# Linear attention with a routed expert layer on one core: four weight chunks, the first rows and small counts placed anew at the turn from attention to the experts

## Chip, cores and metric

The kernel runs on one core of one Trainium2 chip. The metric is the device time of one execution in microseconds (us); the median of three executions counts. All times below are from the hardware's records of such executions.

## What is computed

The first half is a linear attention over 8 batches, 8 heads, 576 positions and 64 channels. The second half takes its output as 4608 tokens of width 512 and sends those with a positive skip score to one of 8 experts. Everything is float32. Cut to what matters:

```
proj = x @ w_phi; proj -= max|proj|          # for q and for k, 128 features
phi  = concat(exp(proj), exp(-proj))         # 256 features
num  = phi_q @ (phi_k^T v);  den = phi_q . sum(phi_k) + 1e-6
x    = (num / den), heads side by side       # [4608, 512]
skip = x @ w_skip > 0;  e = argmax(x @ w_gate);  g = softmax(x @ w_gate)[e]
out  = x;  out[skip] = x + g * (relu(x @ w1[e]) @ w2[e])   # w1 512x1024, w2 1024x512
```

## The kernel before

**Attention.** A loop over time steps `t` runs two streams of units (k and q), one batch after another. TensorE projects and multiplies, VectorE subtracts the maxima, transposes inputs and divides by `den` (lines 490 to 504), ScalarE takes the exponentials, and GpSimd adds partial sums. The order on TensorE, ScalarE and VectorE is the order of the program text nearly to the end of attention; the last steps are ordered by a planner.

**Routing.** After each batch b, `post(b)` makes four things. `choose` picks the expert of each token (one-hot `OH`), its weight through an exponential on ScalarE (line 657) and the reciprocal of its sum on VectorE (line 665), and then stores the right half of the token rows to `xrows` in DRAM (`store_rows`, lines 625 and 627, on SP's queue). `rank` counts the tokens of each expert so far with matmuls over `Stot` and `OH` (line 681 is the first), and `turned` makes from it 128x128 masks `OP` (line 709: two per tile of tokens), on GpSimd for all batches but the last, where VectorE makes them. After batch 5 (`EB`), `pick(0)` and `pick(1)` choose the first two experts from what is counted so far: they subtract the chosen tokens from `Stot` (line 797) and gather 256 rows each from `xrows` with two indirect DMAs on GpSimd's queue (line 213). VectorE's small steps of these generators are slipped in one at a time between the large ones (`hook`); a `yield` is the border of such a step. A third expert is picked later by `pick_third`, in three steps.

**Experts.** The weights come in chunks of 128x1024 float32 through SP's queue (lines 184 and 187): four chunks of `w1`, then four of `w2` for each expert. I number them from one, so chunk one is index 0 in the code. Four buffers take the first twelve chunks. A chunk is split into a high part, written by ScalarE (line 195), and a low part, the difference, written either by VectorE in one instruction or by GpSimd in four pieces of 256 columns (line 200); `CFG['gp']` lists the indices that GpSimd takes. The buffer is free for the next load when both are written. The gathered rows are transposed by TensorE (line 955) and split in the same way into `x` by ScalarE and VectorE (lines 958 and 959). A step of the expert loop is one chunk: `mm1` (lines 1081 to 1084, three products of high and low parts; ScalarE's Relu on line 973, VectorE's difference on line 974) or `mm2` (lines 1095 to 1100). At each step the loop first queues what `before` holds, then splits of coming chunks and the loads behind them, then the matmuls, then what `at` put on that step: the steps of `pick_third` on steps 1 to 3, the last batch's `rank` on step 4, and the steps of `tables` from step 5. One step after an expert's last chunk, VectorE adds the weighted result to the rows (line 1042) and GpSimd scatters them to the output (line 1028).

**Before the loop** stand the loads of chunks one to four, the two gathers, `rows` of the first expert, the splits of chunks one to four with `choose` of the last batch ahead of the fourth, and `rows` of the second expert. There the planner orders the instructions; `tc.issue_after(ins)` only queues what is traced in its block behind `ins`, and only on the engine of `ins`. In the loop the order is that of the program. Before, the last lines ahead of the loop are:

```
if k == FIRST - 1:
    with tc.issue_after(row_last[1].ins):
        for _ in chosen[0]: pass          # choose() of the last batch
...
part(k, nc.gpsimd if k in CFG["gp"] else nc.vector)
rows(order[1])
```

Of the kernel before, what the change touches and what calls it, by code (L numbers as in the profile page):

```python
# [12 lines left out]
AF = mybir.ActivationFunctionType  # L13
ALU = mybir.AluOpType
# [3 lines left out]

P = 128
SLOT = 256  # L20
CFG = {'late': 1, 'gp': (0, 1, 2, 4, 6, 8, 9, 11, 12, 14, 17, 19, 21), 'rows': 9.0, 'tab': (2, 4, 5, 6, 6, 7, 8, 9, 10, 11, 12, 13, 16, 20, 32), 'ql': -2, 'q1': 0, 'vtl': 3, 'at': 6, 'cp': 0, 'seq': ('E', 'E', 'E', 'C', 'C', 'SC', 'C', 'DS', 'C', 'D'), 'lag': (1, 3, 4, 5, 6), 'post': (4, 7, 7), 'man': (8, 79), 'dnow': 0, 'off': 6, 'order': 'EPAZUT', 'direct': (), 'nb': {'K': 1, 'P': 3, 'U': 2, 'O': 2}, 'na': {'K': 1, 'P': 2, 'U': 1, 'O': 2}, 'apools': (('ld', 2), ('hl', 5), ('up', 3), ('zp', 2), ('ep', 7), ('kvp', 6), ('ac', 1), ('xp', 2)), 'mpools': (('rawp', 1), ('mx', 2), ('wseta', 1), ('mo', 2), ('wsetb', 1), ('rawq', 1))}


@with_exitstack
def kernel(
# [12 lines left out]
    nc = tc.nc  # L38
    B, H, S, D = q.shape
    NF = w_phi.shape[1]  # L40
    E = w_gate.shape[1]
# [14 lines left out]
    EB = B - 3  # L56
# [17 lines left out]
    ac = pools["ac"]  # L74
# [38 lines left out]
    Stot = const.tile([P, E], BF16, name="Stot")  # L113
# [145 lines left out]
    with actx:  # L259
        ld, hl, zp, up, ep, kvp, xp = (pools[nm] for nm in ("ld", "hl", "zp", "up", "ep", "kvp", "xp"))  # L260
# [337 lines left out]
        def post(b):  # L598
            last = b == B - 1
# [8 lines left out]
            nt = 4 if b % 2 == 0 else 5  # L608
# [3 lines left out]
            mx = sm("mx", [5])  # L612
            d = sm("d", [5, E])
            ex = sm("ex", [5, E + 1])
# [14 lines left out]
            def choose():  # L629
                for xx, lg, o, n in reversed(parts):  # L630
                    nc.vector.tensor_reduce(
                        out=L[:, o:o + n, :], in_=lg.rearrange("p t h e -> p t e h"), axis=AX.X, op=ALU.add,
                    )
                    yield
                nc.vector.tensor_reduce(out=mx[:, 0:nt], in_=L[:, 0:nt, 0:E], axis=AX.X, op=ALU.max)
                yield
                eng = nc.vector if last else nc.gpsimd
                eng.memset(ex[:, 0:nt, E:E + 1], 1e-9)
                eng.tensor_tensor(out=d[:, 0:nt], in0=L[:, 0:nt, 0:E], in1=bc(mx[:, 0:nt], nt, E), op=ALU.subtract)
                dr = desc.rearrange("p (o e) -> p o e", o=1).broadcast_to([P, nt, E])  # L640
                if last:
                    nc.vector.scalar_tensor_tensor(
                        out=key[:, 0:nt], in0=d[:, 0:nt], scalar=0.0, in1=dr, op0=ALU.is_equal, op1=ALU.mult)
                else:
                    nc.gpsimd.tensor_scalar(out=key[:, 0:nt], in0=d[:, 0:nt], scalar1=0.0, scalar2=None, op0=ALU.is_equal)
                    nc.gpsimd.tensor_tensor(out=key[:, 0:nt], in0=key[:, 0:nt], in1=dr, op=ALU.mult)
                    for _ in range(3):
                        yield
                nc.vector.tensor_reduce(out=km[:, 0:nt], in_=key[:, 0:nt], axis=AX.X, op=ALU.max)
                yield  # L650
                nc.vector.tensor_tensor(out=oh[:, 0:nt], in0=key[:, 0:nt], in1=bc(km[:, 0:nt], nt, E), op=ALU.is_equal)
                yield
                nc.vector.scalar_tensor_tensor(
                    out=OH[:, T, :], in0=L[:, 0:nt, E:E + 1].broadcast_to([P, nt, E]), scalar=0.0, in1=oh[:, 0:nt],
                    op0=ALU.is_gt, op1=ALU.mult,
                )
                nc.scalar.activation(out=ex[:, 0:nt, 0:E], in_=d[:, 0:nt], func=AF.Exp)
                for xx, lg, o, n in parts:
                    nc.scalar.activation(
                        out=xx[:, :, 4 * D + 1:4 * D + 2], in_=sid[:, t0 + o:t0 + o + n].rearrange("p (t o) -> p t o", o=1), func=AF.Copy)  # L660
                yield
                nc.vector.tensor_reduce(out=ss[:, 0:nt], in_=ex[:, 0:nt], axis=AX.X, op=ALU.add)
                yield
                for xx, lg, o, n in parts:
                    nc.vector.reciprocal(out=xx[:, :, 4 * D:4 * D + 1], in_=ss[:, o:o + n].rearrange("p (t o) -> p t o", o=1))
                store_rows()
# [9 lines left out]
            def rank():  # L676
# [3 lines left out]
                r = bank("K" if last else "O")[:, 0:nt * E]  # L680
# [13 lines left out]
                def turned():  # L694
                    if last:
                        count()
                    rm = sm("rm", [5, E])
                    rki = sm("rki", [5], I32)
                    rkp = sm("rkp", [5], I32)
                    nc.vector.tensor_tensor(  # L700
                        out=rm[:, 0:nt], in0=r.rearrange("p (t e) -> p t e", e=E), in1=OH[:, T, :], op=ALU.mult)
                    yield
                    with nc.allow_low_precision(reason="sums of integers below 2**24 written as integers"):
                        nc.vector.tensor_reduce(out=rki[:, 0:nt], in_=rm[:, 0:nt], axis=AX.X, op=ALU.add)
                    yield
                    nc.vector.tensor_scalar(out=rkp[:, 0:nt], in0=rki[:, 0:nt], scalar1=127, scalar2=None, op0=ALU.bitwise_and)  # L706
                    for c in range(2):
                        for t in range(nt):
                            (nc.vector if last else nc.gpsimd).tensor_scalar(  # L709
                                out=OP[:, t0 + t, c, :], in0=iota_p, scalar1=rkp[:, t:t + 1],  # L710
                                scalar2=wcol[:, NT:NT + 1] if c else wcol[:, t0 + t:t0 + t + 1], op0=ALU.is_equal, op1=ALU.mult)
                    yield
                    nc.vector.tensor_scalar(
                        out=RKH[:, T], in0=rki[:, 0:nt], scalar1=7, scalar2=None, op0=ALU.arith_shift_right)
                    yield
                    if not last:
                        count()
                        yield
                    if b > EB:
                        return  # L720
                    for s in range(S):
                        nc.vector.scalar_tensor_tensor(
                            out=rm4[:, 0:nt, :, s], in0=bc(RKH[:, T], nt, E), scalar=float(s), in1=OH[:, T, :],
                            op0=ALU.is_equal, op1=ALU.mult,
                        )
                        if s % 2 == 1:
                            yield
# [46 lines left out]
        def pick(j):  # L774
# [5 lines left out]
            def chosen_pair():  # L780
                mx = sm("mx", [5])[:, 0:1]
# [10 lines left out]
                    out=eid0[:, j:j + 1], in0=km[0:1], scalar1=-1.0, scalar2=float(E), op0=ALU.mult, op1=ALU.add)  # L792
                cs = sm("cs", [E])
                nc.vector.scalar_tensor_tensor(out=cs, in0=cn, scalar=float(SLOT), in1=pk, op0=ALU.min, op1=ALU.mult)
                r = slice(32 * j, 32 * j + 1)
                with nc.allow_low_precision(reason="integers up to 256 are exact"):
                    nc.gpsimd.tensor_tensor(out=Stot[r], in0=Stot[r], in1=cs[r], op=ALU.subtract)
                a4 = acc4.rearrange("p (e s) -> p e s", s=4)
                a2 = acc.rearrange("p (e s) -> p e s", s=2)
                po = pk.rearrange("p (e o) -> p e o", o=1).broadcast_to([P, E, 2])  # L800
# [1 line left out]
                ea = sm("ea", [2], bufs=1)  # L802
                nc.gpsimd.tensor_tensor(
                    out=tp.rearrange("p s e -> p e s"), in0=(a2 if j else a4)[:, :, 0:2], in1=po, op=ALU.mult)
                for _ in range(3):
                    yield
                nc.vector.tensor_reduce(out=ea, in_=tp, axis=AX.X, op=ALU.add)
                places(idg0[:, j], pad0[:, j], ea)
# [8 lines left out]

        rests = []
        chosen = []
        later = []  # L820
        now = [0]
        streams = []
# [7 lines left out]
        man = ExitStack()  # L830
# [455 lines left out]
    def rows(x):  # L1286
        kind, i = x
        xss[x] = split_rows(xgs[x], pad0[:, i] if kind == "E" else ft[:, i, 2:4])


    FIRST = 4
# [16 lines left out]
    def at(k, f):  # L1308
        along.append((k, f))
# [5 lines left out]
    rows(order[0])  # L1315
    for k in range(FIRST):

        if k == FIRST - 1:
            with tc.issue_after(row_last[1].ins):
                for _ in chosen[0]:  # L1320
                    pass
        with ExitStack() as es:
            if k:
                es.enter_context(tc.issue_after(kva_last[0].ins))
            if k == FIRST - 1:
                es.enter_context(tc.issue_after(row_last[0].ins))
                es.enter_context(tc.issue_after(row_last[1].ins))
            part(k, nc.gpsimd if k in CFG["gp"] else nc.vector)
    rows(order[1])
    table = tables()  # L1330
    parts = []

# [2 lines left out]
    one_done = {x: max(k for k, (w, y, c) in enumerate(steps) if y == x and w == 1) for x in order}  # L1335
    TAB = CFG["tab"]
    third = pick_third()
    for k in range(1, 4):
        at(k, lambda: next(third, None))
    at(TAB[1], rests[0])  # L1340
# [114 lines left out]
```

## Time and profile before

| | us |
|---|---|
| median of 3 executions | 590.76 |
| lowest and highest | 590.70, 592.84 |
| the profiled execution | 592.79 |
| its span | 591.0 |
| TensorE busy in the span | 552.0 |
| VectorE busy | 491.4 |
| GpSimd busy | 376.6 |
| ScalarE busy | 327.7 |

The span runs from the first to the last instruction of the profiled execution; 1.8 us of that execution's time lie around it. Starts below are counted from the start of the span. Attention ends and the experts begin at about 320 us.

### The profile page before, as it was taken

The numbers are of one execution on the slowest core, as the hardware profiler recorded it, in microseconds if no ns is written. First come the engines' busy times: TensorE is split into PE (matmuls) and PEld (weight loads), VectorE is DVE, ScalarE is ACT, GpSimd is POOL, SyncE is SP. The second block draws the span as 40 slices with busy tenths as digits, with TensorE's granted clock in tenths as the row PEclk, the third lists the DMA queues.
The fourth block names the chain that finished last, engine by engine and source line by source line (L and its number), as shares of the span: only waits on it lengthen the run. The fifth ranks groups of instructions, "written<-read, shape, count | busy, mean of one in ns | idle before, by whom it ended". The sixth has DMA issues, their size and how long they took to land. (4 is left out here: it accounts for less than half of the span.)

```text
span 591.0 us, 18778 instructions
## 1 busy us (share of the span) xinstructions
PE 552.0 (93%) x7486; PEld 467.6 (79%) x7486; DVE 491.4 (83%) x1056; ACT 327.7 (55%) x649; POOL 376.6 (64%) x434
## 2 busy tenths in 40 slices
PE   5799999999999999999997887999999999999993
PEld 3488888887887878878766867898899988988892
DVE  5789999999999989999876989657779887867840
ACT  4356666665665656556646243444658567546720
POOL 5656468688596794966946655974658582648031
PEclk9999999999999999999999899899999999999998
DMA  8998889697685986813153594788687778877400
GB/s 147 164 159 152 195 185 200 160 188 149 119 212 121 193 168 113 217 46 119 38 183 116 144 366 162 246 290 271 204 284 238 264 261 292 272 214 257 173 20 31
DMA packets 250298, 108.34 MB, mean 183 GB/s; under 512 B 192481, under 2 KB 235617, under 8 KB 250208
## 3 DMA queue, kind: packets, MB, share of 16 engines
q1 hardware_dynamic: 244640, 97.45, 63.3%
q0 software_dynamic: 3200, 9.45, 4.3%
q8 instruction: 60, 0.98, 0.7%
q10 hardware_dynamic: 2368, 0.22, 0.3%
q14 instruction: 30, 0.25, 0.1%
HBM read 83.86 MB, written 24.02 MB: 183 GB/s over the span
## 5 line engine op out<-in xcount | busy, mean ns | idle before, releaser
L200 POOL TENSOR_TENSOR w<-wraw_c,w 128x256 fp32r<-128x256 f32 x108 | 97.1, 931 | 46.6 <-ACT w L195 46.5
L398 POOL TENSOR_TENSOR z<-ek 128x512 f32<-128x512 f32 x64 | 80.8, 1275 | 67.2 <-ACT ek L391 57.7
L200 DVE TENSOR_TENSOR w<-wraw_c,w 128x1024 fp32r<-128x1024 f32 x69 | 98.2, 1439 | 8.8 <-ACT w L195 8.4
L195 ACT ACTIVATE w<-wraw_c 128x1024 fp32r<-128x1024 f32 x96 | 97.8, 1051 | 11.4 <-DMA wraw_c<-in_moe_w_dram 11.4
L370 DVE TENSOR_REDUCE m<-ps_P 128x8 f32<-128x1024 f32 (+3 forms) x86 | 89.6, 1041 | 7.1 <-PE ps_P L357 6.5
L374 DVE TENSOR_TENSOR u<-ps_P,m 128x1024 f32<-128x1024 f32 (+3 forms) x86 | 90.3, 1050 | 4.6
L357 PE MATMUL ps_P<-wsrc,xT 64*64 64x128 f32 x2048 | 72.4, 280 | 10.7 <-DVE xT L334 5.9
L569 PEld LDWEIGHTS ps_O<-kva,eq 128*64 128x64 f32 x2048 | 71.6, 136 | 6.3 <-PE ps_U L412 0.6
L357 PEld LDWEIGHTS ps_P<-wsrc,xT 64*64 64x64 f32 x2048 | 57.9, 135 | 21.2 <-issue 6.9
L569 PE MATMUL ps_O<-kva,eq 128*64 128x74 f32 x2048 | 72.9, 227 | 0.8 <-DVE lgm L504 0.4
L1028 POOL DMA_INDIRECT out_dram<-o,si x22 | 30.4, 1381 | 59.0 <-DVE si L1027 52.4
L434 PE MATMUL ps_K<-ek,v 128*64 128x256 f32 x512 | 67.5, 394 | 0.3 <-ACT ek L391 0.3
L1095 PE MATMUL ps_O<-w,hh 128*128 128x512 f32 x160 | 64.5, 403 | 0.0
L709 POOL TENSOR_SCALAR OP<-iota_p,rkp,wcol 128x128 bf16<-128x128 f32 x62 | 48.3, 793 | 10.6 <-DVE rkp L706 10.5
L418 ACT ACTIVATE eq<-ps_U 128x512 f32<-128x512 f32 x49 | 29.4, 600 | 42.6 <-PE ps_U L412 41.0
L434 PEld LDWEIGHTS ps_K<-ek,v 128*64 128x64 f32 x512 | 34.2, 139 | 20.7 <-issue 7.5
L390 ACT ACTIVATE ek<-u 128x512 f32<-128x512 f32 x64 | 41.2, 644 | 11.5 <-DMA wgs<-in_moe_w_skip_dram 6.3
L1099 PE MATMUL ps_O<-w,hh 128*128 128x512 f32 x120 | 47.4, 395 | 0.0
L1100 PE MATMUL ps_O<-w,hlo 128*128 128x512 f32 x120 | 47.3, 394 | 0.0
L334 DVE STREAM_TRANSPOSE xT<-raw 128x512 f32<-128x512 f32 x64 | 42.7, 685 | 3.1 <-DMA raw<-in_k_dram 3.1
L404 POOL TENSOR_TENSOR z<-z,ekt 64x512 f32<-64x512 f32 x32 | 40.7, 1272 | 1.8
L402 POOL TENSOR_TENSOR z<-z 128x512 f32<-128x512 f32 x32 | 40.6, 1275 | 1.3
(264 smaller groups left out, 1209.3 us busy)
## 6 DMA issues: line engine op xcount, KB each, us to landing
wraw_c<-in_moe_w_dram SPq DMA_DIRECT2D x96, 512.0 KB, 5.0
raw<-in_q_dram SPq DMA_DIRECT2D x64, 144.0 KB, 3.5
raw<-in_k_dram SPq DMA_DIRECT2D x60, 144.0 KB, 3.6
v<-in_v_dram SPq DMA_DIRECT2D x64, 128.0 KB, 3.2
out_dram<-xm SPq DMA_DIRECT2D x16, 512.0 KB, 4.7
xrows<-xm SPq DMA_DIRECT2D x8, 516.0 KB, 4.9
xrows<-xm SPq DMA_DIRECT2D x8, 512.0 KB, 4.3
vt<-in_v_dram SPq DMA_DIRECT2D x32, 32.0 KB, 3.3
```

Source lines behind the costliest of these rows:

```text
L195: nc.scalar.activation(out=hi, in_=raw, func=AF.Copy)
L200: eng.tensor_tensor(out=lo[:, r], in0=raw[:, r], in1=hi[:, r].bitcast(F32), op=ALU.subtract)
L357: nc.tensor.matmul(p[s * 64:s * 64 + 64, hd, (nj + j) * NF:(nj + j + 1) * NF], xT[r, g * P + s * 64:g * P + s * 64 + 64], wsrc[r], start=T ...
L370: nc.vector.tensor_reduce(out=m.rearrange("p (j h) -> p j h", h=2), in_=pv, axis=AX.X, op=ALU.max, apply_absolute_value=True)
L374: nc.vector.tensor_tensor(out=uu[:, 0:2 * nj, :].rearrange("p (j h) f -> p j h f", h=2), in0=pv, in1=m.rearrange("p (j h o) -> p j h o", h ...
L398: zeng.tensor_tensor(out=z, in0=e[:, 0:2, :], in1=e[:, 2:4, :], op=ALU.add)
L434: nc.tensor.matmul(o[hd * 64:hd * 64 + 64, :], u.v[:, 2 * hd + pr, g * D:(g + 1) * D], u.e[i][:, 2 * j + hd, :], start=(g == 0), stop=False,)
L569: nc.tensor.matmul(ov[s * 64:s * 64 + 64, 2 * j + hd, :], e[:, half, j, hd, s * 64:s * 64 + 64], kva[:, half, 2 * pr + hd, :], start=(half ...
L709: (nc.vector if last else nc.gpsimd).tensor_scalar(out=OP[:, t0 + t, c, :], in0=iota_p, scalar1=rkp[:, t:t + 1], scalar2=wcol[:, NT:NT + 1 ...
L1095: nc.tensor.matmul(y[sub], hh[:, t], wh[:, fi, :], start=first, stop=False)
L1099: nc.tensor.matmul(y[sub], hh[:, t], wl[:, fi, :], start=False, stop=False)
L1100: nc.tensor.matmul(y[sub], hlo[:, t], wh[:, fi, :], start=False, stop=last)
```

## The change

Of chunks one to four, GpSimd splits the first and the fourth, and VectorE the second and the third; before, GpSimd split the first three and VectorE the fourth. The splits on VectorE are queued behind the first expert's last row split, and ScalarE's parts of chunks three and four behind the first expert's rows and behind the exponential of the last batch's `choose`. That `choose` is now ahead of chunk three. The second expert's rows move into the expert loop, to the end of step 4, ahead of the last batch's `rank`. VectorE subtracts from `Stot` in both picks, the second pick waits one small step in place of three, and of the eight masks of the last batch but one VectorE makes two.

```diff
-CFG = {'late': 1, 'gp': (0, 1, 2, 4, 6, 8, 9, 11, 12, 14, 17, 19, 21), ...
+CFG = {'late': 1, 'gp': (0, 3, 4, 6, 8, 9, 11, 12, 14, 17, 19, 21), ...
...
-                nc.scalar.activation(out=ex[:, 0:nt, 0:E], in_=d[:, 0:nt], func=AF.Exp)
+                ex_last[0] = nc.scalar.activation(out=ex[:, 0:nt, 0:E], in_=d[:, 0:nt], func=AF.Exp)
...
-                            (nc.vector if last else nc.gpsimd).tensor_scalar(
+                            (nc.vector if last or b > EB and t == 0 else nc.gpsimd).tensor_scalar(
...
-                    nc.gpsimd.tensor_tensor(out=Stot[r], in0=Stot[r], in1=cs[r], op=ALU.subtract)
+                    nc.vector.tensor_tensor(out=Stot[r], in0=Stot[r], in1=cs[r], op=ALU.subtract)
...
-                for _ in range(3):
+                for _ in range(3 - 2 * j):
                     yield
...
-        if k == FIRST - 1:
+        if k == 2:
             with tc.issue_after(row_last[1].ins):
                 for _ in chosen[0]:
                     pass
         with ExitStack() as es:
             if k:
                 es.enter_context(tc.issue_after(kva_last[0].ins))
-            if k == FIRST - 1:
+                es.enter_context(tc.issue_after(row_last[1].ins))
+            if k >= 2:
                 es.enter_context(tc.issue_after(row_last[0].ins))
-                es.enter_context(tc.issue_after(row_last[1].ins))
+                es.enter_context(tc.issue_after(ex_last[0].ins))
             part(k, nc.gpsimd if k in CFG["gp"] else nc.vector)
-    rows(order[1])
...
+    at(4, lambda: rows(order[1]))
     for k in range(1, 4):
         at(k, lambda: next(third, None))
```

## Rows read from the trace of the kernel before

**Rows 1.** Busy time by stretch: microseconds, busy per engine, granted TensorE clock, DMA

```profile
330.00:340.00 10.00, 8.16 (x55) 7.92 (x55) 9.15 (x21) 3.59 (x6) 4.21 (x7) 0.83 0.57 161
...
360.00:370.00 10.00, 6.58 (x40) 5.69 (x40) 9.38 (x24) 2.61 (x4) 8.62 (x11) 0.87 0.36 127
370.00:380.00 10.00, 10.00 (x39) 8.28 (x39) 7.70 (x12) 4.50 (x5) 9.51 (x11) 0.79 0.61 195
...
470.00:480.00 10.00, 10.00 (x52) 8.28 (x51) 8.28 (x16) 7.08 (x14) 7.22 (x8) 1.00 0.92 338
```

**Rows 2.** Timeline of TensorE: start, duration, instruction, idle before and its releaser

```profile
314.04 0.18 PE L681 MATMUL ps_O<-Stot,ones_b 128*128 128x32 bf16 x1 [1.57 <-POOL Stot L797]
...
322.64 0.38 PE L1081 MATMUL ps_P<-x,w 128*128 128x256 f32 x1 [1.31 <-ACT x L958]
...
335.42 0.39 PE L1081 MATMUL ps_P<-x,w 128*128 128x256 f32 x1 [1.84 <-DVE hlo L974]
...
345.00 0.19 PE L681 MATMUL ps_K<-Stot,ones_b 128*128 128x40 bf16 x1 [2.20 <-DVE tp_e L253]
...
353.57 0.28 PE L1081 MATMUL ps_P<-x,w 128*128 128x256 f32 x1
...
366.10 0.38 PE L1084 MATMUL ps_P<-x,w 128*128 128x256 f32 x1 [1.33 <-POOL w L200]
...
368.05 0.58 PE L1084 MATMUL ps_P<-x,w 128*128 128x256 f32 x1 [0.60 <-POOL w L200]
```

**Rows 3.** Timeline of GpSimd, the same columns

```profile
313.80 0.19 POOL L797 TENSOR_TENSOR Stot<-Stot,cs 1x8 bf16<-1x8 bf16 x1 [5.47 <-DMA xg<-xrows,idg]
...
316.84 6.22 POOL L709 TENSOR_SCALAR OP<-iota_p,rkp,wcol 128x128 bf16<-128x128 f32 x8
323.04 8.35 POOL L200 TENSOR_TENSOR w<-wraw_c,w 128x256 fp32r<-128x256 f32 x12
...
361.16 1.09 POOL L1028 DMA_INDIRECT out_dram<-o,si  x1 [6.12 <-DVE si L1027]
...
363.58 7.47 POOL L200 TENSOR_TENSOR w<-wraw_c,w 128x256 fp32r<-128x256 f32 x8
```

**Rows 4.** Timeline of VectorE, the same columns

```profile
315.72 0.17 DVE L692 TENSOR_TENSOR Stot<-Stot,st 128x8 bf16<-128x8 bf16 x1
...
324.13 8.34 DVE L200 TENSOR_TENSOR w<-wraw_c,w 128x1024 fp32r<-128x1024 f32 x1
...
332.50 1.27 DVE L959 TENSOR_TENSOR x<-ps_U,x 128x512 fp32r<-128x512 f32 x2
...
337.82 1.74 DVE L200 TENSOR_TENSOR w<-wraw_c,w 128x1024 fp32r<-128x1024 f32 x1
...
343.44 0.69 DVE L974 SCALAR_TENSOR_TENSOR hlo<-ps_P,hh 128x512 fp32r<-128x512 f32 x1 [2.34 <-ACT hh L973]
...
345.80 1.21 DVE L200 TENSOR_TENSOR w<-wraw_c,w 128x1024 fp32r<-128x1024 f32 x1
...
348.00 5.73 DVE L709 TENSOR_SCALAR OP<-iota_p,rkp,wcol 128x128 bf16<-128x128 f32 x10
...
360.05 0.75 DVE L1042 SCALAR_TENSOR_TENSOR o<-ps_O,xg 128x512 f32<-128x512 f32 x1
```

**Rows 5.** Waits of VectorE from 343 to 372 us: total, times, longest

```profile
DVE hlo L974 <- ACT hh L973: 2.3, 1, 2.3
DVE w L200 <- ACT w L195: 0.2, 1, 0.2
```

**Rows 6.** Timeline of ScalarE, the same columns

```profile
318.66 2.95 ACT L195 ACTIVATE w<-wraw_c 128x1024 fp32r<-128x1024 f32 x3
...
341.87 1.06 ACT L195 ACTIVATE w<-wraw_c 128x1024 fp32r<-128x1024 f32 x1 [4.37 <-DMA wraw_c<-in_moe_w_dram]
```

**Rows 7.** Timeline of SP's queue, the same columns

```profile
334.70 0.37 SPq L625 DMA_DIRECT2D xrows<-xm  x1
...
335.89 1.35 SPq L187 DMA_DIRECT2D wraw_c<-in_moe_w_dram  x2
```

More of the change, by code (lines that the diff above doesn't have):

```diff
@@ L20 @@
 SLOT = 256
-CFG = {'late': 1, 'gp': (0, 1, 2, 4, 6, 8, 9, 11, 12, 14, 17, 19, 21), 'rows': 9.0, 'tab': (2, 4, 5, 6, 6, 7, 8, 9, 10, 11, 12, 13, 16, 20, 32), 'ql': -2, 'q1': 0, 'vtl': 3, 'at': 6, 'cp': 0, 'seq': ('E', 'E', 'E', 'C', 'C', 'SC', 'C', 'DS', 'C', 'D'), 'lag': (1, 3, 4, 5, 6), 'post': (4, 7, 7), 'man': (8, 79), 'dnow': 0, 'off': 6, 'order': 'EPAZUT', 'direct': (), 'nb': {'K': 1, 'P': 3, 'U': 2, 'O': 2}, 'na': {'K': 1, 'P': 2, 'U': 1, 'O': 2}, 'apools': (('ld', 2), ('hl', 5), ('up', 3), ('zp', 2), ('ep', 7), ('kvp', 6), ('ac', 1), ('xp', 2)), 'mpools': (('rawp', 1), ('mx', 2), ('wseta', 1), ('mo', 2), ('wsetb', 1), ('rawq', 1))}
+CFG = {'late': 1, 'gp': (0, 3, 4, 6, 8, 9, 11, 12, 14, 17, 19, 21), 'rows': 9.0, 'tab': (2, 4, 5, 6, 6, 7, 8, 9, 10, 11, 12, 13, 16, 20, 32), 'ql': -2, 'q1': 0, 'vtl': 3, 'at': 6, 'cp': 0, 'seq': ('E', 'E', 'E', 'C', 'C', 'SC', 'C', 'DS', 'C', 'D'), 'lag': (1, 3, 4, 5, 6), 'post': (4, 7, 7), 'man': (8, 79), 'dnow': 0, 'off': 6, 'order': 'EPAZUT', 'direct': (), 'nb': {'K': 1, 'P': 3, 'U': 2, 'O': 2}, 'na': {'K': 1, 'P': 2, 'U': 1, 'O': 2}, 'apools': (('ld', 2), ('hl', 5), ('up', 3), ('zp', 2), ('ep', 7), ('kvp', 6), ('ac', 1), ('xp', 2)), 'mpools': (('rawp', 1), ('mx', 2), ('wseta', 1), ('mo', 2), ('wsetb', 1), ('rawq', 1))}
 @with_exitstack
@@ L819 @@
         chosen = []
+        ex_last = [None]
         later = []
```

## Prediction

> **What bounds the kernel now.** I began with busy time by stretch [rows 1]. In the eleven windows of 10 us from 370 to 480 (the first and the last stand there, none is below 9.75) TensorE is always busy; ahead of them two windows miss 1.84 and 3.42 us. So the experts run at TensorE's pace once they run, and what the turn loses is not won back. The granted clock is below 1.00 in the same stretches: 0.83, 0.87 and 0.79, time at 1.2 instead of 2.4 GHz.
>
> TensorE's timeline [rows 2] names the waits: 1.57 us for GpSimd's subtraction from `Stot`, 1.31 for the first rows, 1.84 and 2.20 for small VectorE results, and last the stretch up to 368.05, where each piece of a low part on GpSimd is waited for. This last wait counts, since nothing behind it is idle. Followed back it gives a chain:
>
> - The pieces are those of chunk twelve, at 363.58, right behind the first expert's scatters at 361.16, which waited 6.12 us for VectorE [rows 3].
> - VectorE comes to these rows (line 1042) at 360.05. From 343.44 it has stood still only once, for 0.2 us [rows 4, 5]: its queue is full, and whatever starts it at 343.44 sets the end.
> - At 343.44 it waited 2.34 us for ScalarE, whose Relu stood behind the high part of chunk seven, which waited for its load until 341.87 [rows 4, 6].
> - That load was issued at 335.89, behind the row stores of the last batch at 334.70 [rows 7]. The stores need the last reciprocal of `choose`.
> - `choose` stood behind one split on VectorE, of chunk four: 8.34 us from 324.13, where the same instruction takes 1.21 at 345.80 [rows 4]. GpSimd's twelve pieces of chunks one to three ran from 323.04 for 8.35 us [rows 3]; VectorE was done 1.1 us behind the last of them.
>
> So an excess of 8.34 - 1.21 = 7.1 us on VectorE is carried, wait by wait, to 368.05.
>
> **The change part by part.**
>
> *Subtraction from `Stot` on VectorE.* GpSimd's took 0.19 us, but began 5.47 us late: it waited for the landing of the first gather [rows 3]. On VectorE the nearest row is the addition to the same tile, 0.17 us [rows 4]. Neither operand is what the gather writes, so I take the wait to go with GpSimd's queue, and TensorE's 1.57 us with it [rows 2]. If the wait moves along, VectorE stands up to 5.47 us with the last divisions of attention queued behind it: bounds 0.17 and 5.6 us.
>
> *The second pick two steps earlier* issues its gather earlier on a queue that no longer waits; its rows are needed in step 4 only. Worth nothing, covered by the first four chunks; without that cover it could cost at most the 5.47 us again.
>
> *Two masks on VectorE.* GpSimd's eight take 6.22 us, 0.78 each [rows 3]; six end 1.6 us earlier. VectorE's cost 5.73 / 10 = 0.57 each [rows 4], so 1.15 us ahead of the last divisions. Of TensorE's 1.57 us I therefore keep 1.0 at the end of attention (bounds 0.4 and 1.57).
>
> *First rows ahead of chunk three.* ScalarE made three high parts in 2.95 us before these rows [rows 6]; now two, 0.98 less. Together with the 1.0 the first rows are split some 1.7 us earlier (not 2.0, as TensorE's transposes must also have come).
>
> *The splits.* GpSimd has chunk one only in this stretch, 8.35 / 3 = 2.8 us, nearly all of it done before VectorE's split of chunk two. `choose` runs in a gap of GpSimd, since ScalarE makes chunks three and four only behind its exponential. VectorE gets one split more, 1.21 us. Its excess of 7.1 us goes. Two bounds: in a short overlap with four pieces a split took 1.74 us [rows 4], 0.5 more; against a row of pieces without end it stands for the whole row, 2.8 us for chunk four and as much again for chunk five.
>
> Here a page of the Trainium skill differs from the trace. The row shows a split held through twelve GpSimd instructions. "SBUF — State Buffer", section "Who interferes with whom", says that a VectorE instruction with two SBUF inputs and a GpSimd instruction that reads SBUF exclude each other for the whole of one instruction. By that the split would have waited for one piece, 0.7 us, and there would be no 7.1 us to win; the measured 8.34 decides. The rule speaks against the change where it puts VectorE's splits beside GpSimd's chunks four and five; by it they would lose 0.7 us each there, which lies inside the bounds of my case.
>
> *Start of the loads.* The stores at 334.70 came after the excess, the second rows' pair of splits (1.27 us, now moved away) and the choice. They are now earlier by 1.7 + 7.1 + 1.3, less the two splits that now stand ahead of them, 2.4: 7.7 us; chunk three's buffer is free in the same microsecond. The load of chunk seven moves with the stores. Bounds: 6 (0.5 lost at each of three overlaps) and 9 (load ahead of the stores, which saves their 1.2 us on SP [rows 7]). Its transfer keeps 341.87 - 335.89 = 6.0 us, in which stores share the DMA as before.
>
> *Second rows in step 4.* On TensorE they fall where it now waits for the third pick. On ScalarE they are covered. On VectorE they come into the full queue: 1.27 us [rows 4], unless they slip into the wait for the Relu, which they can't, as they are queued behind the third pick. VectorE works through to line 1042 as before.
>
> *Sum at 368.05:* -7.7 + 1.3 = -6.4. TensorE itself comes earlier, since the waits of 1.31, 1.84 and part of 2.20 us go too, and only waits longer for chunk twelve. The slow clock around 368 I leave as it is; if one stretch of it goes, [rows 1] give 0.13 x 10 to 0.21 x 10 us more. So -6.4, with -4.5 to -9 for this case. The profiled execution of 592.79 (span 591.0 and 1.8 around it) would become 586.4. It lies 2.0 above the median of 590.76; the prediction is for the median: **584.4 us**, 581.8 to 586.3.
>
> **The rivals.**
>
> *A shorter gain: chunk three's split is locked out again.* Its high part and that of chunk four come from ScalarE one after the other, 0.98 us apart. If VectorE reaches its split after GpSimd began on chunk four, it may stand for that row, 2.8 us, or through chunk five too, 5.6. For it: the row of 8.34. Against it: `choose` leaves VectorE little to do in just that microsecond. The `Stot` wait moved to VectorE falls here too. Gain 6.4 - 2.8 = 3.6 or 0.8: 587.2 or 590.0.
>
> *No change: the new wait is the load.* If SP's planner keeps the load of chunk seven behind something that has not moved, or its transfer meets the output stores that also come earlier, VectorE still starts at about 343 and the excess turns into idle time. For it: VectorE did idle 2.34 us there. Against: the load's row follows the stores within 1.2 us. Time 590.5.
>
> *Slower: VectorE's queue is longer.* Place: from the last divisions to line 1042. The added split 1.21, masks 1.15 and moved rows 1.27 make 3.6 us on the queue that sets the end. It decides where the locked-out time reaches the 7.1 us that it was before: chunk one's row for the split of chunk two, and four and five for chunk three, 3 x 2.8 = 8.4 us. Then the sum is 8.4 - 7.1 + 3.6 = 4.9, less the 1.7 of the earlier start: +3.2, 594.0. For it: GpSimd's pieces before stood in just such a row. Against it: between chunk one and chunk four GpSimd must wait for the exponential.
>
> **How the numbers follow.** The main case 0.62, the shorter gain 0.19, no change 0.10, slower 0.09. A measurement of this kernel tells about 0.5%, 3.0 us, from no change. Faster by more: 0.62 and two thirds of 0.19, 0.74; within: the rest of that and 0.10, 0.16; slower: 0.09, rounded up to 0.10. The range runs from 580.5 (the bound of 9 with a stretch of the slow clock) to 590.0 (the shorter gain's far end) and leaves out "no change", "slower" and little else, about 2 in 10.
>
> **What the profile of the changed kernel would show.** No wait of TensorE for `Stot`; VectorE's two first splits at 1.2 to 1.8 us each; row stores on SP near 327 and the load of chunk seven within 2 us behind them; VectorE's line 974 after its longest wait near 336; line 1042 near 354; TensorE at the last piece of chunk twelve near 361.7, after a longer wait there than before. A split of 3 us or more means the shorter gain. Line 1042 still near 360 means no change. The prediction is wrong if the wait for chunk twelve is set by something else than VectorE's queue, or if TensorE is no longer unbroken behind it.

## The result and the profile after

The changed kernel takes 586.55 us (median of five, 585.3 to 587.32) against 590.76 of the kernel before (five runs of the same occasion, 589.98 to 592.84): ratio 0.991, 95% interval 0.9883 to 0.9937. By the ratio it is faster by 0.9%, some 5.3 us; the two medians lie 4.2 us apart. 584.4 was predicted, with a range of 580.5 to 590.0 that holds the result; the likeliest case's own range ended 0.25 us below it, at 586.3. The profiled execution took 587.23, its span is 585.5. Behind line 820 the lines of the changed kernel are one higher: 1043 is 1042 of before.

Busy time by stretch, the columns of [rows 1]:

```profile
330.00:340.00 10.00, 10.00 (x77) 9.36 (x76) 8.27 (x24) 5.79 (x8) 8.06 (x11) 1.00 0.91 266
340.00:350.00 10.00, 10.00 (x56) 8.48 (x55) 9.59 (x30) 4.25 (x4) 5.76 (x8) 1.00 1.01 352
350.00:360.00 10.00, 7.99 (x65) 7.58 (x63) 9.52 (x30) 5.58 (x7) 4.90 (x7) 1.00 0.63 225
360.00:370.00 10.00, 9.05 (x34) 7.50 (x35) 9.62 (x20) 4.50 (x5) 9.51 (x11) 0.66 0.56 185
370.00:380.00 10.00, 10.00 (x60) 8.76 (x59) 6.24 (x10) 4.04 (x5) 9.59 (x11) 1.00 0.74 257
```

TensorE no longer misses anything from 330 to 350; what it misses now lies from 350 to 362. The 0.83 of 330 to 340 has gone with the waits there. The slow clock behind 360 has not: one window at 0.66 (3.4 us lost in granted clock) stands for 0.87 and 0.79 in [rows 1] (1.3 + 2.1).

The rows that answer the chain, from its start. VectorE, to be held against [rows 4]:

```profile
308.80 0.16 DVE L797 TENSOR_TENSOR Stot<-Stot,cs 1x8 bf16<-1x8 bf16 x1
...
316.39 0.66 DVE L709 TENSOR_SCALAR OP<-iota_p,rkp,wcol 128x128 bf16<-128x128 f32 x2
...
323.77 1.28 DVE L200 TENSOR_TENSOR w<-wraw_c,w 128x1024 fp32r<-128x1024 f32 x1
...
327.03 0.13 DVE L665 RECIPROCAL xt<-ss 128x1 f32<-128x1 f32 x1
...
327.58 1.23 DVE L200 TENSOR_TENSOR w<-wraw_c,w 128x1024 fp32r<-128x1024 f32 x1 [0.31 <-ACT w L195]
...
336.35 0.69 DVE L975 SCALAR_TENSOR_TENSOR hlo<-ps_P,hh 128x512 fp32r<-128x512 f32 x1 [0.83 <-ACT hh L974]
...
339.54 1.29 DVE L960 TENSOR_TENSOR x<-ps_U,x 128x512 fp32r<-128x512 f32 x2
...
341.81 3.15 DVE L709 TENSOR_SCALAR OP<-iota_p,rkp,wcol 128x128 bf16<-128x128 f32 x10
...
353.77 0.75 DVE L1043 SCALAR_TENSOR_TENSOR o<-ps_O,xg 128x512 f32<-128x512 f32 x1
```

Both first splits take what such a split takes alone, and the last reciprocal of `choose` ends between them, at 327.2. SP's queue [rows 7] follows it:

```profile
327.15 0.37 SPq L625 DMA_DIRECT2D xrows<-xm  x1
...
328.83 3.08 SPq L187 DMA_DIRECT2D wraw_c<-in_moe_w_dram  x2
```

GpSimd [rows 3]: six masks, one chunk, a pause until ScalarE has made the high part, and the scatters 6.28 us earlier.

```profile
316.46 4.75 POOL L709 TENSOR_SCALAR OP<-iota_p,rkp,wcol 128x128 bf16<-128x128 f32 x6 [4.01 <-DVE rkp L706]
321.19 2.78 POOL L200 TENSOR_TENSOR w<-wraw_c,w 128x256 fp32r<-128x256 f32 x4
328.57 9.48 POOL L200 TENSOR_TENSOR w<-wraw_c,w 128x256 fp32r<-128x256 f32 x12 [4.61 <-ACT w L195]
...
354.88 1.09 POOL L1029 DMA_INDIRECT out_dram<-o,si  x1 [5.11 <-DVE si L1028]
...
357.30 7.49 POOL L200 TENSOR_TENSOR w<-wraw_c,w 128x256 fp32r<-128x256 f32 x8
```

TensorE [rows 2]: the wait for `Stot` is gone and so are those of 1.84 and 2.20 us; three gaps that the profile puts down to nothing ("issue") have come; the wait for chunk twelve still stands last, its last piece at 361.79.

```profile
307.92 0.77 PE L465 MATMUL ps_O<-aug,kvs 128*128 128x146 f32 x4 [0.71 <-issue]
...
312.29 0.40 PE L548 MATMUL ps_O<-kva,eqt 128*64 128x74 f32 x5 [0.38 <-issue]
313.01 0.38 PE L548 MATMUL ps_O<-kva,eqt 128*64 128x74 f32 x5 [0.32 <-issue]
...
314.51 0.19 PE L681 MATMUL ps_O<-Stot,ones_b 128*128 128x32 bf16 x1
...
323.07 0.39 PE L1082 MATMUL ps_P<-x,w 128*128 128x256 f32 x1 [0.74 <-ACT x L959]
...
359.84 0.42 PE L1085 MATMUL ps_P<-x,w 128*128 128x256 f32 x1 [1.35 <-POOL w L200]
...
361.79 0.58 PE L1085 MATMUL ps_P<-x,w 128*128 128x256 f32 x1 [0.41 <-POOL w L200]
```

### The profile page after: what moved, and what is told of

Its sections match the earlier page's. It is cut to its first block, busy times and chain, and to the rows that moved or that the text cites. A ratio compares the mean times of both kernels' runs of the same rounds, so it can differ in the third digit from the quotient of the medians.

```text
span 585.5 us, 18767 instructions
## 1 busy us (share of the span) xinstructions
PE 550.1 (94%) x7486; PEld 465.8 (80%) x7486; DVE 488.0 (83%) x1061; ACT 328.2 (56%) x649; POOL 375.4 (64%) x426
## 5 line engine op out<-in xcount | busy, mean ns | idle before, releaser
L200 DVE TENSOR_TENSOR w<-wraw_c,w 128x1024 fp32r<-128x1024 f32 x70 | 92.7, 1339 | 8.7 <-ACT w L195 8.3
L370 DVE TENSOR_REDUCE m<-ps_P 128x8 f32<-128x1024 f32 (+3 forms) x86 | 89.6, 1042 | 7.1 <-PE ps_P L357 6.7
L1029 POOL DMA_INDIRECT out_dram<-o,si x22 | 31.6, 1434 | 56.1 <-DVE si L1028 49.2
L709 POOL TENSOR_SCALAR OP<-iota_p,rkp,wcol 128x128 bf16<-128x128 f32 x60 | 46.8, 794 | 14.5 <-DVE rkp L706 14.5
```

The costliest lines, as they stand in the source:

```text
L200: eng.tensor_tensor(out=lo[:, r], in0=raw[:, r], in1=hi[:, r].bitcast(F32), op=ALU.subtract)
L370: nc.vector.tensor_reduce(out=m.rearrange("p (j h) -> p j h", h=2), in_=pv, axis=AX.X, op=ALU.max, apply_absolute_value=True)
L709: (nc.vector if last or b > EB and t == 0 else nc.gpsimd).tensor_scalar(out=OP[:, t0 + t, c, :], in0=iota_p, scalar1=rkp[:, t:t + 1], scal ...
```

## Experiments

Each was timed in five rounds against the kernel before. "In us" is the ratio's distance from 1 on 590.76.

| kernel | median | ratio, interval | in us |
|---|---|---|---|
| the change, again | 586.09 | 0.9899, 0.9875 to 0.9922 | -6.0 |
| splits and order only | 587.75 | 0.9934, 0.9914 to 0.9955 | -3.9 |
| counts and masks only | 589.65 | 0.9965, 0.9948 to 0.9982 | -2.1 |
| all four chunks by GpSimd | 593.49 | 1.0031, 1.0015 to 1.0047 | +1.8 |
| the change, second rows back | 584.13 | 0.9891, 0.9868 to 0.9913 | -6.4 |
| the change, second pick late | 585.29 | 0.9916, 0.9897 to 0.9935 | -5.0 |
| the change, old engines | 585.97 | 0.9928, 0.9908 to 0.9947 | -4.3 |
| the change, masks back | 588.41 | 0.9939, 0.9918 to 0.9959 | -3.6 |
| before, row cut (memsets moved away) | 592.26 | 1.0009, 0.9994 to 1.0024 | +0.5 |
| before, row cut | 587.58 | 0.9947, 0.9927 to 0.9968 | -3.1 |
| before, split ahead of scatters | 590.66 | 0.9980, 0.9967 to 0.9993 | -1.2 |
| the change, split ahead of scatters | 581.44 | 0.9870, 0.9844 to 0.9895 | -7.7 |

**The change again.** No edit.

> The changed kernel once more, nothing else. In its first profile TensorE stood still for 0.71, 0.38 and 0.32 us between 306 and 313 us for nothing that the profile shows, which the kernel before did not. If that was chance, it is gone or elsewhere here and the experts' first matmul (line 1082) starts near 321 instead of 323.07; if the change causes it, it stands in the same place with about 1.4 us. The time is 585 to 588 either way.

The time repeats. The gaps of TensorE are fewer but there, 0.35 and 0.32 us at 311.56 and 312.29, and chunk one begins at 321.98 in place of 323.07.

**Parts alone.** The splits with their order, and the rows of the second expert where they were:

```diff
-CFG = {'late': 1, 'gp': (0, 1, 2, 4, 6, ...
+CFG = {'late': 1, 'gp': (0, 3, 4, 6, ...
...
-        if k == FIRST - 1:
+        if k == 2:
...
+            if k >= 2:
+                es.enter_context(tc.issue_after(row_last[0].ins))
+                es.enter_context(tc.issue_after(ex_last[0].ins))
```

> Before, with only the new division and order of chunks one to four and of choose (masks, Stot, picks and the second expert's rows as before). My theory, that the 8.34 us split is carried along a chain to line 1042: stores near 328, line 1042 at 354 to 355, 4 to 5.5 us faster. The rival that GpSimd's late subtraction from Stot and the masks make the gain: within 1.5 us of before. The rival that the moved rows make it: within 1.5 us of before too.

The counts, the masks and the second pick alone:

```diff
-                            (nc.vector if last else nc.gpsimd).tensor_scalar(
+                            (nc.vector if last or b > EB and t == 0 else nc.gpsimd).tensor_scalar(
...
-                    nc.gpsimd.tensor_tensor(out=Stot[r], in0=Stot[r], in1=cs[r], op=ALU.subtract)
+                    nc.vector.tensor_tensor(out=Stot[r], in0=Stot[r], in1=cs[r], op=ALU.subtract)
...
-                for _ in range(3):
+                for _ in range(3 - 2 * j):
```

> Before, with only the subtraction from Stot and two masks on VectorE and the second pick two steps earlier. My theory: TensorE's wait of 1.57 us for Stot goes, the split of 8.34 us stays (GpSimd's row only starts some 2 us earlier), so at most 2 us faster, 0.5 to 2. The rival that these counts make the gain: 3 us or more.

The splits gave 3.9 (4 to 5.5 expected), the counts 2.1 (0.5 to 2 expected); together 6.0, the whole. With the splits alone the stores came at 329.96, where near 328 was expected. In both the first split on VectorE still stood to the end of GpSimd's row. VectorE's and GpSimd's timelines with the counts alone (the row ends at 329.40, the split 1.08 later):

```profile
324.81 5.67 DVE L200 TENSOR_TENSOR w<-wraw_c,w 128x1024 fp32r<-128x1024 f32 x1
```
```profile
321.05 8.35 POOL L200 TENSOR_TENSOR w<-wraw_c,w 128x256 fp32r<-128x256 f32 x12
```

With the splits alone GpSimd's eight masks put chunk one's four pieces beside the split of chunk two, which took 3.30.

**No split left on VectorE.** In the kernel before, GpSimd takes chunk four as well.

```diff
-CFG = {'late': 1, 'gp': (0, 1, 2, 4, 6, ...
+CFG = {'late': 1, 'gp': (0, 1, 2, 3, 4, 6, ...
```

> Before, with chunk four split by GpSimd as well, so that no split on VectorE meets GpSimd's row; order, counts and rows as before. My theory: choose is no longer held, the stores come near 327 to 328 instead of 334.7, and line 1042 moves from 360 by 4 to 6 us; chunk four's low part is ready at about 334.3, so TensorE loses little: 3 to 5.5 us faster. The rival that it takes the new order and the shorter row on GpSimd: no faster than before, as the row is now 16 pieces, 11.1 us.

A miss, and the most telling run: slower. With no split there, the hold fell on the first small operation of `choose`, which takes 0.20 elsewhere. VectorE and GpSimd:

```profile
325.11 0.06 DVE L638 MEMSET ex<- 128x5 f32 x1
...
326.00 8.31 DVE L639 TENSOR_TENSOR d<-L,mx 128x40 f32<-128x40 f32 x1
```
```profile
323.11 11.14 POOL L200 TENSOR_TENSOR w<-wraw_c,w 128x256 fp32r<-128x256 f32 x16
```

The operation ends at 334.31, the row of sixteen pieces at 334.25. So the wait at this place belongs not to the split, but to the first VectorE operation with two operands in SBUF that meets GpSimd's unbroken row.

**The row cut.** In the kernel before, a memset of one element between GpSimd's pieces. In the first attempt it wrote a tile of its own:

```diff
+            if eng is nc.gpsimd and i < 4:
+                nc.gpsimd.memset(brk, 0)
```

> The kernel before, and nothing of the change: GpSimd only gets a one-element memset after each of its pieces of chunks one, two and four (and of chunk nought). In the trace of before VectorE's split of chunk three took 8.34 us, to the end of GpSimd's row of twelve pieces, where such a split alone takes 1.2 to 1.3. If the hold lasts as long as GpSimd's operations of two SBUF operands follow each other without a break, VectorE gets in after the first memset: its split takes at most 2.5 us, the choice ends 5 to 6 us earlier, the stores come near 328 to 329, and the time falls by what the splits alone brought or a little less, 2 to 4.5 us: 586 to 588.5, ratio 0.9925 to 0.9965. If the hold is a matter of the place (the operands, the banks, the traffic of loads) and not of the unbroken row, the split takes 8 us or more again, and the time is that of before or up to 0.5 us over it for the twelve to sixteen memsets of 0.09 us.

(This text and that of the run with the old engines count chunks by the code's index, from nought; the memsets stand behind the pieces of nought, one and two.) The framework put all twelve memsets at the kernel's start, so the row stayed whole, the split took 7.40, to the row's end, and the run repeats before: ratio 1.0009. In the second attempt each memset overwrites an element that its piece has read, and the next piece is queued behind it:

```diff
+                if cut[0] is not None and eng is nc.gpsimd and i < 4:
+                    es.enter_context(tc.issue_after(cut[0].ins))
...
+            if eng is nc.gpsimd and i < 4:
+                cut[0] = nc.gpsimd.memset(raw[0:1, a:a + 1], 0.0)
```

> The kernel before, and nothing of the change: behind each of GpSimd's twelve pieces of chunks one to three (numbered from one) stands a memset of one element of the buffer that this piece has just read, so that it cannot move away, and the next piece stands behind it. (In the experiment row_broken the twelve memsets had been placed at the kernel's start, so that the row there was whole and the run a repeat of before.) In before VectorE's split of chunk four took 8.34 us, to the end of the row, where such a split takes 1.2 to 1.3 alone. If the hold lasts as long as GpSimd's operations of two SBUF operands follow each other without a break, VectorE gets in after the first memset: its split takes at most 2.5 us, or some 5 if it has to give way again at each piece; the stores come at 328 to 332 in place of 334.7, and the time falls by 1.5 to 4.5 us: 586.5 to 589.5, ratio 0.9925 to 0.9975. If the hold is a matter of the place (operands, banks, the traffic of loads), the split takes 8 us or more again and the time is that of before, or up to 1.5 us over it for twelve memsets that each wait for the piece ahead of them.

The row cut came out as its first theory expected. VectorE's split of chunk four, and GpSimd's row around it:

```profile
323.93 1.54 DVE L204 TENSOR_TENSOR w<-wraw_c,w 128x1024 fp32r<-128x1024 f32 x1
```
```profile
323.66 0.73 POOL L204 TENSOR_TENSOR w<-wraw_c,w 128x256 fp32r<-128x256 f32 x1
324.45 0.09 POOL L206 MEMSET wraw_c<- 1x1 f32 x1
324.50 1.55 POOL L204 TENSOR_TENSOR w<-wraw_c,w 128x256 fp32r<-128x256 f32 x1
326.12 0.09 POOL L206 MEMSET wraw_c<- 1x1 f32 x1
326.17 0.72 POOL L204 TENSOR_TENSOR w<-wraw_c,w 128x256 fp32r<-128x256 f32 x1
```

VectorE waits for one piece, goes ahead, and GpSimd's next piece stands aside once: 1.55 for 0.73. The stores come at 327.97, the line that adds the results (1042 of before) at 356.5 instead of 360.05, and the time falls by 3.1 us with none of the change made. Whether the memset or its wait for the piece ahead lets VectorE in, this run does not separate.

**Parts of the change undone.** The second expert's rows ahead of the loop again (`rows(order[1])` back, `at(4, ...)` out):

> The changed kernel with one part undone: the second expert's rows go back to where they were, ahead of the sharp queue's loop instead of into it. If the time came from VectorE's choice no longer standing behind GpSimd's row and from the counts, this move is worth its own 1.3 us on VectorE at most: within 1 us of the changed kernel, 585.5 to 588, ratio to before 0.989 to 0.994. If the moved rows carry a large share (the rows at 315.72 in the trace of before stand ahead of the choice), the stores come at least 1.3 us later than the 327.15 of the changed kernel and the time goes back to that of the splits alone or later, 588 or more, ratio over 0.994.

Their move is worth nothing that can be measured. The second pick with its three steps (`range(3)`):

> The changed kernel, but with as many steps between the second pick's counts and its places as before, so that the second gather is issued 2 to 4 us later than the 310.2 of the changed kernel. Theory: TensorE's gaps for nothing the profile shows (1.4 us between 306 and 314 in the changed kernel) come because its next 16 KB packet of instructions stands behind two gathers in a row (the packet began at 314.6, as the gathers ended at 314.8; in before it began at 311.8). Then with the gathers apart the packet begins by 313, the gaps between 311 and 314 go or shrink below 0.3 us, and the first matmul of chunk one starts up to 0.7 us earlier; the end gains no more than that: 585.5 to 587. Rival: the gaps belong to the length of TensorE's loop code at that place whatever the DMA does; then they stand at the same instructions, 0.7 us in all. If the gather being early is itself worth something at the end, this run is 1 us or more slower than the changed kernel.

The gaps of TensorE from 311 to 314 are gone, and the time is that of the change. But they are also gone with the rows back and with the old engines, where the two gathers follow each other as closely; so the gathers alone do not make them. The old engines in the new order (`gp` of before):

> The changed kernel with the splits given back to the engines of before (chunks one, two and four by GpSimd, three by VectorE), in the new order. If what counts is that GpSimd has no unbroken row beside the choice, the row of eight pieces from 321 (5.6 us) catches VectorE's first operations of two SBUF operands once: the choice ends 1 to 4 us later than the 327.1 of the changed kernel, and the time lies between the two kernels, 587.5 to 590, ratio 0.993 to 0.998. If the order alone brought the time (the choice ahead of VectorE's first split), the choice ends at 327 to 328 and the time is that of the changed kernel, 586 to 587, ratio 0.990 to 0.993.

GpSimd's row from 318.29 for 5.57 caught `choose`'s first operation for 1.91 us in place of 0.20, and no more; the stores came at 324.74 and the time is that of the change. The time between the two kernels that I expected did not come: with the counts and the rows, the new order reaches the time of the change, and which engine splits which of the four chunks adds nothing that can be measured; 1 to 2 us would lie within the intervals. The masks back on GpSimd (`nc.vector if last else nc.gpsimd`):

> The changed kernel with one part undone: the two first masks of each such group go back from VectorE to GpSimd (0.33 us each on VectorE, 0.78 on GpSimd by the traces). GpSimd's row of chunk one then starts and ends 1.5 us later. If, as in the changed kernel, that row is off the path that ends last, the time is that of the changed kernel within 0.7 us, ratio 0.989 to 0.993. If GpSimd sets the start (chunk one's pieces late for TensorE, the row running into VectorE's split as in the splits alone, where the split took 3.30 us), it is 1 to 2 us slower, ratio 0.993 to 0.9945.

The second case came true: GpSimd's row starts at 322.88 instead of 321.19, VectorE's split of chunk two at 323.84 takes 2.90, and the time rises by some 1.7 to 2.4 us against the change and its repeat, whose intervals overlap with this one. By these ratios the two masks would be most of what the counts brought.

**What is left.** The wait for chunk twelve is still there after the change, since its split is queued behind the scatters. The split ahead of them, in the changed kernel:

```diff
-            for f in [f for s, f in before if s == k]:
-                f()
+            if k != 8:
+                for f in [f for s, f in before if s == k]:
+                    f()
...
-            while nxt < len(steps) and nxt <= k + 6 and (nxt <= k + 1 or parted[nxt] <= T[k] + 1.0):
+            while nxt < len(steps) and nxt <= k + 6 and (nxt <= k + 1 or parted[nxt] <= T[k] + 1.0 or k == 8 and nxt <= 11):
...
+            if k == 8:
+                for f in [f for s, f in before if s == k]:
+                    f()
```

> The changed kernel with GpSimd's split of chunk twelve queued ahead of the first expert's two scatters instead of behind them. In the changed kernel the scatters start at 354.9 and wait 5 us for the table's end on VectorE (353.8), the split runs from 357.3, and TensorE waits 3.0 us for its four pieces from 358.1 on and then stands 6.8 us at half clock. If that wait is what is left of the stall the prediction followed, the split starts near 350, TensorE does not wait for it and the half clock from 360 on goes: 3 to 6 us faster than the changed kernel, 580.5 to 583.5, ratio 0.982 to 0.988. Rival: the scatters then come 5 to 6 us later and hold the buffers or the gathers behind them (the next gathers are queued on GpSimd after the split), so that the wait only changes its place: 585.5 to 589. A second rival: the half clock stands whatever the wait; then the gain is 1.5 to 3 us.

The same edit in the kernel before:

> The kernel before, with only the order of the fastest experiment on GpSimd: chunk twelve's split ahead of the first expert's two scatters, no part of the change. If the change and this order take away two ends of one stall, the order alone already takes TensorE's wait for chunk twelve (3.7 us with the last piece at 368.05 in before) and the half clock behind it: 3 to 6 us faster than before, 584.5 to 587.5, ratio 0.990 to 0.995, and with the change it adds to 9 us. If the split has no earlier place in before (its load or the high part from ScalarE comes too late there, since the loads hang on the stores at 334.7), the gain is under 1 us and the order pays only behind the change.

Behind the change it is the fastest kernel of the study: 581.44, where the three other forms of the change on the same occasion took 584.13 to 585.97. The stretches with it:

```profile
350.00:360.00 10.00, 8.22 (x57) 6.99 (x55) 9.59 (x27) 5.33 (x7) 6.30 (x8) 1.00 0.45 161
360.00:370.00 10.00, 9.05 (x43) 7.17 (x43) 9.72 (x18) 3.53 (x6) 9.52 (x9) 1.00 0.66 216
```

The slow clock from 360 to 370 is gone with the wait for chunk twelve (1.00 for 0.66). Its waits of TensorE from 340 to 380:

```profile
PE ps_O L1100 <- POOL w L200: 1.4, 3, 0.7
PE ps_P L1082 <- DVE hlo L975: 1.2, 1, 1.2
```

In the kernel before, the edit brought 1.2 us where I expected 3 to 6. The wait for chunk twelve (3.4 us) went there too, but the earlier ones stand; its waits of TensorE from 330 to 380:

```profile
PE ps_K L681 <- DVE tp_e L253: 2.5, 1, 2.5
PE ps_P L1081 <- DVE hlo L974: 1.7, 1, 1.7
PE ps_O L1099 <- POOL w L200: 1.4, 3, 0.6
```

Why it brought so little is not settled. The wait that it took away was no smaller than in the change (3.4 us against 3.0). But the slow clock, gone behind 360, came to 340 to 350, where the granted clock is 0.83 in place of 1.00, and the 1.4 us for line 1099 are new, as they are behind the change. With the change the same edit is worth 1.2 to 3.4 us by the ratios (0.987 against 0.9891 to 0.9928), where 3 to 6 were expected; that it is worth more there than in before lies within the intervals and is not shown.

## Why the prediction was right, step by step

- **The chain.** Its times came as said: splits at 1.28 and 1.23, stores at 327.15 (near 327 was said), the load of chunk seven 1.7 us behind them (within 2), line 975 at 336.35 (near 336), line 1043 at 353.77 (near 354), TensorE's last piece of chunk twelve at 361.79 (361.7). At that point -6.26 stands against the sum of -6.4. (From 330 to 370 three windows miss time, not two: 340 to 350 misses 2.20, the wait that the prediction names next. The sum does not use the count.)
- **One link of it no longer carries.** In the prediction the stores and the load of chunk seven set VectorE's start at line 975. In the changed kernel ScalarE's part of chunk seven follows a Relu at once, 4.6 us behind the issue of the load (6.0 was said), and the Relu ahead of 336.35 waits for TensorE's fourth chunk:

```profile
332.84 0.60 ACT L974 ACTIVATE hh<-ps_P 128x512 fp32r<-128x512 f32 x1 [1.45 <-PE ps_P L1085]
333.46 1.06 ACT L195 ACTIVATE w<-wraw_c 128x1024 fp32r<-128x1024 f32 x1
335.72 0.60 ACT L974 ACTIVATE hh<-ps_P 128x512 fp32r<-128x512 f32 x1 [1.20 <-PE ps_P L1085]
```

TensorE has no gap from 324 to 357, so its own pace from chunk one sets 336.35. That both ways lead to 336 is luck. The start came 7.09 us earlier (7.7 was said), and VectorE's way from there to line 1043 grew by 0.81 (1.3 was said). The longer wait for chunk twelve did not come either: 3.0 us against 3.4, since TensorE reached it 6.0 us earlier and the pieces 6.28.

- **The excess of 7.1 us on VectorE** is shown to be GpSimd's unbroken row at the turn: moved to a 128x40 operation it took 8.31 us, and the row cut took the split to 1.54 us. The Trainium skill, "SBUF — State Buffer", section "Who interferes with whom", has the exclusion hold for one instruction. At the turn the whole rows, with 8.34, 8.31 and 5.67 us, decide against it. Where the row is cut the traces agree with it, each side waiting for one instruction of the other, and they agree in uncut rows too. In the changed kernel VectorE's split of chunk six, beside the chunks of which the prediction spoke, got in amid the twelve pieces from 328.57 and lost 0.6 us, while GpSimd's piece at 332.86 took 1.72 us:

```profile
332.19 1.79 DVE L200 TENSOR_TENSOR w<-wraw_c,w 128x1024 fp32r<-128x1024 f32 x1
```

In the kernel before a split did so amid the eight pieces from 363.58 [rows 3]:

```profile
364.07 1.40 DVE L200 TENSOR_TENSOR w<-wraw_c,w 128x1024 fp32r<-128x1024 f32 x1 [0.24 <-ACT w L195]
```

- **The counts.** The wait for `Stot` went, as said (0.16 us on VectorE, no gather waited for). VectorE's masks cost 0.33 each and not 0.57; the ten of [rows 4] stood beside a row of GpSimd, and the same ten take 3.15 us in the changed kernel, where none stands there. By the run with the masks back, what the two masks brought is that GpSimd's row ends before VectorE's split; the prediction had the earlier end, 1.6 us, but no price for it.
- **First rows 1.7 us earlier** did not come in this trace: TensorE begins chunk one at 323.07 against 322.64 [rows 2], 2.1 us off, with 1.4 us of gaps that were not foreseen. Without the gaps it came: from the first pick's reduction (line 807) to chunk one it is 17.95 us in the kernel before, 18.34 in the change, 17.95 in its repeat, and 16.21 in each of the four forms of the change that have no gaps. The sum held because the term "less the two splits that now stand ahead", 2.4, was wrong too. Chunk four's own 1.21 left VectorE, chunk two's 1.28 came in its place, and chunk three's (327.58) stands behind `choose`: nothing was added there. 2.1 lost and 2.4 won cancel, which is luck, and the stores moved by 7.55 us where 7.7 was said.
- **The second rows in step 4** took 1.29 us on VectorE (1.27 was said); with the rows back ahead of the loop the end is the same.
- **From -6.26 to -5.5 in the span:** in TensorE's waits behind 362 the wait for `hsum` (a sum that VectorE makes in later steps) grew from 2.2 to 2.6, and 0.5 for line 1043 and 0.3 of "issue" are new, 1.2 in all, of which the span keeps 0.8. The slow clock behind 360 stayed, as assumed. This, and the profiled execution of before lying 2.0 above its median where that of the change lies 0.7 above, is the distance to 584.4.
- **The rivals.** The shorter gain is real where GpSimd is later: splits of 2.90 and 3.30 us with the masks back and with the splits alone. "No change" and "slower" did not occur: ScalarE did not wait for the load of chunk seven, and no row of GpSimd stood beside the choice.

## What to carry to other kernels

Before moving work off an engine, look in the trace for its first operation with two SBUF operands that lies beside an unbroken row of such operations on GpSimd. If it lasts to the end of the row, as at the turn of this kernel, its size does not matter, and taking it away hands the bill to the next one; in other rows of the same traces VectorE got in after one piece, so the duration has to be read and not assumed. Change the order so that the row has a pause there, or cut the row, before changing who does what. When a stall is carried along a chain, look as well for work that is queued behind its late end without need (here a split behind scatters): that wait was the one left once the stall was gone.

## What was not expected of the hardware

- A VectorE operation of 128x40 stood for 8.31 us beside GpSimd's row, and a one-element memset of 0.09 us between the pieces, with the next piece queued behind it, was enough to let VectorE in. Beside GpSimd's row from 344.00 for 5.76 in the changed kernel small VectorE operations took 0.67 us each, one piece. Why that row, and those at 328.57 and 363.58, let VectorE in after one piece and those at the turn do not stays open. It is not the turn alone: with the split ahead of the scatters, in the changed kernel, a VectorE split at 387.17 stood for 6.40 us, to the end of a row of eight pieces from 386.89.
- TensorE's "issue" gaps from 306 to 314, 1.4 us in the changed kernel, are there in some kernels and absent in others of nearly the same program. In those with gaps just ahead of 314, the change, its repeat, the counts alone and the masks back, the next 16 KB packet on the instruction queue began at 314.0 to 315.0; in the four forms of the change without (rows back, late pick, old engines, split first), at 310.4 to 312.8. What makes it late is open.
